# Expert 0's second product computed directly with 512-column products, the other experts' by seven block products

## The chip, the cores and the metric

The kernel runs on one NeuronCore of a Trainium2 chip. Its engines are TensorE (PE, matrix products), VectorE (DVE), ScalarE (ACT), GpSimd (POOL) and SyncE (SP, which here only issues transfers). Each runs its own instructions in the order in which the program wrote them; between engines, semaphores make one wait for another. The metric is the device time of one execution in microseconds (us), lower is better; the time of a version is the median of its runs.

## What is computed

The reference is a chunked attention followed by a mixture of eight experts whose weights come from a Sinkhorn routing:

```python
for c in range(nc):                      # attention: 4 batches, 8 heads, 768 rows, chunks of 32
    scores = scale * q_c @ k_full.T      # k_full: 8 memory rows and a window of 56
    out[c] = softmax(scores) @ v_full
x = out as [3072, 512]                   # all heads side by side
P = exp(x @ w_gate - max)                # then 8 rounds of row and column scaling
for e in range(8):
    h = np.maximum(x @ w1[e], 0.0)       # [3072, 1024]
    ye = h @ w2[e]                       # [3072, 512]
    out += P[:, e:e + 1] * ye
```

All data are float32. The kernel splits every operand of the expert products into a high and a low float16 part and multiplies three of the four pairs (`PASSES`), so one float32 product costs three float16 products.

## The kernel before

**Units.** The 3072 rows are cut into `NU` = 6 units of 512 rows (`TU` = 4 row tiles of 128). The work on the experts is a sequence of 48 units: expert 0 on units 0 to 5, expert 1 on units 5 to 0, and so on (L312). The hidden layer of a unit is computed in `FP` = 4 parts (`hidden`, L1275), the second product in two pairs of row tiles (`output`, L1473).

**Seven block products.** Both products are done as a 2 x 2 block product with seven multiplications in place of eight (`P1` to `P7`, L1244), which needs sums of blocks of both operands. For weights `cut` (L539) makes the sums on POOL (`ws`) and splits the plain blocks and the sums into high and low parts (`split`, L457: the high part on ACT, the low part on DVE). For the attention's result x the function `build` (L970) does the same, with its sums in `xt`, partly on DVE, partly on POOL. For the hidden layer the sums are made from the relu of the four blocks: `rr` and its negative on ACT (L1350, L1360), three steps on DVE (L1372), the high parts on ACT (L1383, L1408), the low parts on DVE (L1416) and, for the first `ASIDE` = 8 units, the low parts of the sums on POOL (L1432). Within a product, blocks gather in PSUM banks (px, py, pz and yx, yy, yz); ACT reads some of them into `q` or `y` (L1304, L1508), and DVE adds these to others (L1314, L1528).

**One stage with two kinds of work.** While expert 0 is computed, the attention still runs: 24 blocks of 128 rows, four to a unit. Each takes loads of q, k and v, transposes, scores (sp, L865), a softmax on DVE, ACT and POOL (the last step is L915), a transpose (ta) and the product with v (xp, L948). After every fourth block `build` makes the next unit's x and `logits` its router scores. After the last one comes the routing (L1135 to L1222), a chain between DVE and PE, and with it the first weights of expert 1.

**Who decides the order.** The kernel doesn't write its instructions in program order. Every step is a task of a `Plan` (L86) with an engine, an estimated cost and a due time (`prio`); `Plan.run` plays the tasks through with these estimates, on each engine takes the earliest due of those ready, and writes the instructions in the order that results. Where this leaves a hole on PE while the attention runs, `pad` (L119) fills it with products on a constant (`warm`, L376) that nobody reads. Due times follow from `begin(n)` (L314): START + TURN for each of the first five units, then UNIT for each, and `outputs_at(n)` (L319), half a TURN after a unit's begin for units 0 to 3. The attention's due times (`needed`, L625) follow START and AHEAD alone. `hidden` and `output` write their products through `product` (L1250), which makes each wait for the one before it through `last_pe`. For units 0 to 3 a unit's outputs come behind its hidden layer; from unit 5 on, the outputs of unit n - 1 come between the first and the second half of the hidden layer of unit n (L1682).

**Buffers.** A `Ring` (L53) hands out a few buffers in turn, in the order of the program's text; whoever takes one waits for all users of the tile that lay in it before. Of `ss` there are two, for the sums of h and for the attention's `xt`; of `c` there are two, for the three blocks of h before their split. x has two, h and the cut weights four each (more after the attention). PSUM gives `main` four banks.

**Results.** An expert adds its part to `acc`, which lies in DRAM between experts (`akeep`). Expert 0 stores its part unscaled, and expert 1 scales it when it fetches it (L1459).

Of the kernel before, what the change touches and what calls it, by code (L numbers as in the profile page):

```python
# [12 lines left out]
F32 = mybir.dt.float32  # L13
I32 = mybir.dt.int32
AF = mybir.ActivationFunctionType
ALU = mybir.AluOpType
# [69 lines left out]
class Plan:  # L86
# [13 lines left out]
    def add(self, eng, cost, fn, deps=(), prio=0.0, bufs=(), takes=None, frees=None, dma=0.0):  # L100
        t = Task()
        t.eng, t.cost, t.fn, t.prio, t.takes, t.frees = eng, cost, fn, prio, takes, frees
        t.ready, t.end, t.then, t.n, t.dma = 0.0, None, [], len(self.tasks), dma
        if dma:
            t.cost = cost * ISSUE
        before = {id(d): d for d in deps if d is not None}
        for b in bufs:
            assert not b.closed
            before.update({id(d): d for d in b.before})
            b.users.append(t)  # L110
        t.left = len(before)
        for d in before.values():
            d.then.append(t)
        if frees is not None:
            frees.left += 1
        self.tasks.append(t)
        return t
# [86 lines left out]
def tile_chunked_attn_sinkhorn_moe(  # L204
# [27 lines left out]
    nc = tc.nc  # L232
    P = 128
    B, H, S, D = q.shape
    NM = mem_k.shape[2]
    N, DM = out.shape
    E, _, F = w1.shape
# [11 lines left out]
    FP = F // P // 2  # L249
    GT = 256  # L250
# [3 lines left out]
    TU = UT // P  # L254
    TH = GT // P
    DH = DM // 2
    NBLK = B * NB
    SCALE = 1.0 / float(D) ** 0.5
    DOWN = 2.0**-HSHIFT
# [6 lines left out]
    hl = ctx.enter_context(tc.tile_pool(name="hl", bufs=1))  # L266
    stage = ctx.enter_context(tc.tile_pool(name="stage", bufs=1))
    apool = ctx.enter_context(tc.tile_pool(name="apool", bufs=1))
    comb = ctx.enter_context(tc.tile_pool(name="comb", bufs=1))
# [30 lines left out]
    akeep = [dram.tile([P, DM], F32, name=f"akeep_{T}") for T in range(NT)]  # L300

    plan = Plan()
    add = plan.add
# [2 lines left out]
    plan.free["two"] = [(0.0, 6)]  # L306


    START, TURN, UNIT, AHEAD = 50.0, 74.0, 36.7, 62.0
    ASIDE = NU + 2  # L310
    STEP = UNIT / 56
    units = [(e, u if e % 2 == 0 else NU - 1 - u) for e in range(E) for u in range(NU)]  # L312
# [39 lines left out]
    def buf(kind, pool, shape, dtype, name, slot=None):  # L352

        return rings[kind].take(
            lambda k: pool.tile(shape, dtype, tag=f"{kind}_{k}", name=name), slot
        )

    def operands(kind, shape, name):

        near = {"w1": wl1, "w2": wl2, "h": hl}[kind]  # L360
        return rings[kind].take(
            lambda k: (near if k < 4 else late[kind]).tile(
                shape, F16, tag=f"{kind}_{k}", name=name
            )
        )

    def bank(group, shape, name):
        return Bank(group, lambda b: ps.tile(shape, F32, tag=f"b{b}", name=name))

    FIRM = 200.0  # L370
# [86 lines left out]
    def split(dst, src, s, deps, prio, costs, bufs=()):  # L457

        a = add(
            "ACT",  # L460
            costs[0],
            lambda: nc.scalar.activation(dst(0), src(), AF.Copy, scale=s),  # L462
            deps,
            prio - 1.0,
            bufs,
        )
        b = add(
            "DVE",
            costs[1],
            lambda: nc.vector.scalar_tensor_tensor(  # L470
                dst(1), src(), s, dst(0), op0=ALU.mult, op1=ALU.subtract
            ),
            [a],
            prio,
            bufs,
        )
        return b
# [4 lines left out]
    wo = {}  # L482
    known = {}
# [54 lines left out]

    def cut(e, fp, which, st, ld, prio):  # L539
        s = sw[:, e, which - 1 : which]  # L540
        ws = buf(
            "ws", comb, [P, 4, 2, P] if which == 1 else [P, 4, DH], F32, f"ws{which}_{e}_{fp}"
        )
        eng = nc.gpsimd

        def tt(i, a, b, op):
            return lambda: eng.tensor_tensor(ws.t[:, i], a(), b(), op=op)  # L547

        def part(i):
            return lambda: ws.t[:, i]  # L550

        if which == 1:
            a11, a12 = lambda: st.t[:, 0, 0:2], lambda: st.t[:, 0, 2:4]
            a21, a22 = lambda: st.t[:, 1, 0:2], lambda: st.t[:, 1, 2:4]
            ops = [
                (0, a21, a22, ALU.add),
                (1, part(0), a11, ALU.subtract),
                (2, a11, a21, ALU.subtract),
                (3, a12, part(1), ALU.subtract),
            ]  # L560
            shape = [P, 2, 7, 2, P]
        else:
            b11, b12 = lambda: st.t[:, 1, 0:DH], lambda: st.t[:, 1, DH:DM]
            b21, b22 = lambda: st.t[:, 0, 0:DH], lambda: st.t[:, 0, DH:DM]
            ops = [
                (0, b12, b11, ALU.subtract),
                (1, part(0), b22, ALU.subtract),
                (2, b22, b12, ALU.subtract),
                (3, b21, part(1), ALU.add),
            ]  # L570
            shape = [P, 2, 7, DH]
        o = operands("w1" if which == 1 else "w2", shape, f"w{which}_{e}_{fp}")
        sums = []
        for op in ops:
            sums.append(add("POOL", 0.95, tt(*op), [ld] + sums[-1:], prio - 5, [st, ws]))
        deps = [known[e, which], ld]
        if which == 1:
            parts = [
                (
                    lambda j: o.t[:, j, 0:2].rearrange("p o k f -> p (o k) f"),  # L580
                    lambda: st.t[:, 0],
                    (0.72, 0.85),
                ),
                (lambda j: o.t[:, j, 2], a22, (0.5, 0.65)),
            ]
            flat = "p o k f -> p (o k f)"
        else:
            parts = [
                (
                    lambda j: o.t[:, j, 1:3].rearrange("p o d -> p (o d)"),  # L590
                    lambda: st.t[:, 0],
                    (0.72, 0.85),
                ),
                (lambda j: o.t[:, j, 0], b11, (0.5, 0.65)),
            ]
            flat = "p o d -> p (o d)"
        done = [split(d, src, s, deps, prio - 2, costs, [st, o]) for d, src, costs in parts]
        done.append(
            split(
                lambda j: o.t[:, j, 3:7].rearrange(flat),  # L600
                lambda: ws.t.rearrange(flat),
                s,
                deps + sums,
                prio,
                (1.15, 1.28),
                [ws, o],
            )
        )
        wo[e, fp, which] = (o, done)
# [636 lines left out]
    PASSES = ((0, 0), (0, 1), (1, 0))  # L1246
    now = [0.0, 1.0]
# [27 lines left out]
    def hidden(e, u, fp, hs, use_at, aside):  # L1275

        nm = f"{e}_{u}_{fp}"
# [3 lines left out]
        def run(dst, op, more, deps, takes=None):  # L1281
            a, b = op
            return product(
                dst,
                lambda: [
                    (w.t[:, wl, a, kt], x.t[:, xl, b, kt]) for kt in range(2) for wl, xl in PASSES
                ],
                more,
                deps,
                [w, x],  # L1290
                takes,
            )

        def psum(name):
            b = bank("main", [P, GT], f"{name}_{nm}")
            b.kind = "h"
            return b
# [12 lines left out]
        def plus(o, src, q, deps, last=True):  # L1310
# [10 lines left out]
            )  # L1321

        h = operands("h", [P, 2, 7, GT], f"h_{nm}")
        c = buf("c", comb, [P, 3, GT], F32, f"c_{nm}")
        px, py, pz = psum("px"), psum("py"), psum("pz")
        t1 = run(px, P1, False, made, px)
        q1, r1 = read(px, "q1", t1)
# [2 lines left out]
        c11 = plus(2, py, q1, [t2, r1])  # L1330
# [8 lines left out]
        c22 = plus(0, px, q5, [t7, r5], last=False)  # L1339
        yield  # L1340
        t3 = run(pz, P3, True, [r5])
        c12 = plus(1, pz, q6, [t3, r6])
        yield
        t4 = run(px, P4, True, [c22])

        rr = lambda i: h.t[:, 1, 3 + 2 * i : 5 + 2 * i].rearrange("p a n -> p (a n)").bitcast(F32)
        r = add(
# [5 lines left out]
            [h],  # L1353
            frees=px,
        )
        at = min(use_at, now[0] + 12.0)
        rn = add(
            "ACT",
            0.4,
# [6 lines left out]
        ss = buf("ss", comb, [P, 4, GT], F32, f"ss_{nm}")  # L1366

        def rsum(cost, dst, src, other, op, deps, extra=()):
# [11 lines left out]
        hi = add(  # L1380
            "ACT",
            0.85,
            lambda: nc.scalar.activation(h.t[:, 0, 0:3], c.t, AF.Relu),  # L1383
            [c11, c22, c12],
            at - 6.0,
            [h, c],
        )
# [33 lines left out]
                op0=ALU.max,  # L1421
                op1=ALU.subtract,
# [17 lines left out]
    akept = {}  # L1440
# [32 lines left out]
    def output(n, t, hs):  # L1473
# [135 lines left out]
            )  # L1609
        yield  # L1610


    def run(*gens):

        gens = list(gens)
        while gens:
            for g in list(gens):
                if next(g, StopIteration) is StopIteration:
                    gens.remove(g)

    def outputs(n, hs):
        run(*[output(n, t, hs) for t in range(TU // 2)])

    def first_weights():
# [19 lines left out]
        dma=0.3,  # L1644
# [3 lines left out]
    for n, (e, u) in enumerate(units):  # L1648
# [29 lines left out]
        hs = hidden_of[n] = []  # L1678
# [21 lines left out]
        if n >= NU and n % NU < NU - 2:  # L1700
# [16 lines left out]
                        dma=7.0,  # L1717
# [36 lines left out]
```

## Time and profile before

| | us |
|---|---|
| time, median of 3 runs | 2022.2 (2020.78 to 2023.33) |
| time of the profiled execution | 2018.44 |
| its span | 2016.6 |
| PE busy | 1956.9 |
| DVE busy | 1541.5 |
| ACT busy | 1065.8 |
| POOL busy | 625.0 |

The profile is of one execution. Its page has the busy time of each engine, the span in 40 slices of about 50 us with the busy share of each engine in tenths, the chain of work that ended last, and groups of instructions with a line of the kernel, an engine, what is written from what, a count, the busy time and the mean. A busy PE isn't a PE at its peak: products overlap, and a product's own length contains its passage through the array. A timeline lists instructions of one engine in order; its columns are start, length, engine, line, operation, tiles and count, and in brackets the idle time ahead of the first with what ended it. A table of windows gives the busy time of each engine in stretches of the span; restricted to a line or a tile, it gives those instructions alone.

### The profile page before, as it was taken

What the parts mean: (1) busy time and instruction counts of PE and PEld (TensorE: products, weight loads), DVE (VectorE), ACT (ScalarE), POOL (GpSimd) and SP (SyncE); (2) the same over time, 40 slices, a digit from 0 to 9 for tenths busy, and PEclk for the clock granted to TensorE, in tenths of its full rate; (3) what the DMA queues carried; (4) which work ended last, traced back from release to release, by engine and by line L of the source; (5) the groups of instructions that cost most, each with busy time, mean ns of one, the idle gap of its engine ahead of it and who ended that gap; (6) DMA issues with size and microseconds to landing.
All of it is one profiled execution on the core that took longest, in us unless ns stands there. A gap on an engine that the chain in (4) does not pass through costs nothing.

```text
span 2016.6 us, 48811 instructions
## 1 busy us (share of the span) xinstructions
PE 1956.9 (97%) x20193; PEld 1735.6 (86%) x20193; DVE 1541.5 (76%) x2522; ACT 1065.8 (53%) x2094; POOL 625.0 (31%) x608
## 2 busy tenths in 40 slices
PE   8889999989999999999999999999999999999999
PEld 7777878768888888888888888888888888888887
DVE  5997766798777886688867986788858977777564
ACT  4645655545555654554645555545536455465353
POOL 2543313246312422143223421242313521242112
PEclk9989999989999999999999999999999999999999
DMA  7664543025422544226423444146332453232321
GB/s 166 176 180 119 130 130 98 38 69 185 161 111 71 177 142 139 82 94 208 144 85 111 152 142 152 48 126 220 100 121 85 152 176 113 65 119 80 120 80 64
DMA packets 242191, 248.56 MB, mean 123 GB/s; under 512 B 114736, under 2 KB 176176, under 8 KB 237616
## 3 DMA queue, kind: packets, MB, share of 16 engines
q1 hardware_dynamic: 241328, 245.31, 38.2%
q8 instruction: 158, 2.59, 0.5%
q14 instruction: 65, 0.53, 0.1%
q10 hardware_dynamic: 640, 0.13, 0.0%
HBM read 184.04 MB, written 61.34 MB: 122 GB/s over the span
## 4 chain that ended last, share of the span: by engine, by line
PE 85%; DVE 10%; issue 2%; DMA 1%; POOL 1%; ACT 1%; SPq 0%; ACTq 0%; DVEq 0%; POOLq 0%
PE yx L1257 24%; PE px L1257 22%; PE yz L1257 12%; PE pz L1257 11%; PE yy L1257 6%; PE py L1257 6%; DVE ss L1372 3%; PE xp L948 2%; DVE c L1314 1%; DVE h L1416 1%; DVE w L470 1%; PE sp L865 1%; DVE x L470 1%; PE ta L938 1%; POOL h L1432 0%
## 5 line engine op out<-in xcount | busy, mean ns | idle before, releaser
L1257 PEld LDWEIGHTS <-w 128*128 128x128 f16 x8064 | 790.3, 98 | 120.0 <-issue 25.9
L1257 PEld LDWEIGHTS <-h 128*128 128x128 f16 x8064 | 789.8, 98 | 95.7 <-ACT h L1383 1.0
L1257 PE MATMUL px<-x,w 128*128 128x256 f16 x4608 | 566.7, 274 | 19.3 <-DVE c L1314 19.0
L1537 POOL TENSOR_TENSOR acc<-acc,y 128x256 f32<-128x256 f32 x252 | 274.6, 1095 | 891.5 <-ACT y L1512 888.4
L1257 PE MATMUL yx<-w,h 128*128 128x256 f16 x4608 | 538.4, 273 | 1.4 <-ACT h L1383 0.7
L1304 ACT ACTIVATE q<-px 128x256 f32<-128x256 f32 x384 | 146.3, 382 | 317.8 <-PE px L1257 311.4
L1257 PE MATMUL pz<-x,w 128*128 128x256 f16 x2304 | 284.8, 273 | 3.2 <-DVE c L1314 2.8
L1257 PE MATMUL yz<-w,h 128*128 128x256 f16 x2304 | 268.9, 273 | 0.0
L1383 ACT ACTIVATE h<-c 128x768 f16<-128x768 f32 x192 | 160.9, 838 | 126.0 <-DVE c L1314 125.8
L1408 ACT CAST h<-ss 128x1024 f16<-128x1024 f32 x192 | 199.1, 1040 | 39.6 <-DVE ss L1372 39.6
L1432 DVE TENSOR_TENSOR h<-ss,h 128x1024 f16<-128x1024 f32 x160 | 205.7, 1297 | 3.8 <-ACT h L1408 3.8
L1372 DVE SCALAR_TENSOR_TENSOR ss<-c,ss 128x256 f32<-128x256 f32 x384 | 199.9, 521 | 9.4
L1416 DVE SCALAR_TENSOR_TENSOR h<-c,h 128x768 f16<-128x768 f32 x192 | 196.0, 1024 | 12.8 <-ACT h L1383 12.7
L1314 DVE SCALAR_TENSOR_TENSOR c<-px,q 128x256 f32<-128x256 f32 x192 | 78.4, 422 | 111.7 <-PE px L1257 111.0
L1372 DVE SCALAR_TENSOR_TENSOR ss<-c,h 128x512 f32<-128x512 f32 x192 | 147.9, 770 | 7.5 <-ACT h L1360 7.3
L1257 PE MATMUL py<-x,w 128*128 128x256 f16 x1152 | 142.6, 274 | 0.0
L1512 ACT ACTIVATE y<-yx,pscale 128x256 f32<-128x256 f32 x168 | 79.6, 474 | 113.5 <-PE yx L1257 109.9
L1257 PE MATMUL yy<-w,h 128*128 128x256 f16 x1152 | 133.9, 273 | 0.0
L1314 DVE SCALAR_TENSOR_TENSOR c<-py,q 128x256 f32<-128x256 f32 x192 | 80.9, 424 | 63.8 <-PE py L1257 48.4
L1432 POOL TENSOR_TENSOR h<-ss,h 128x1024 f16<-128x1024 f32 x32 | 73.0, 2286 | 118.2 <-ACT h L1408 94.4
L462 ACT ACTIVATE w<-ws,sw 128x1024 f16<-128x1024 f32 x64 | 73.1, 1142 | 68.2 <-POOL ws L547 68.2
L470 DVE SCALAR_TENSOR_TENSOR w<-ws,sw,w 128x1024 f16<-128x1024 f32 x64 | 88.7, 1386 | 20.0 <-ACT w L462 20.0
(129 smaller groups left out, 1772.5 us busy)
## 6 DMA issues: line engine op xcount, KB each, us to landing
x<-xkeep SPq DMA_DIRECT2D x28, 1792.0 KB
akeep<-acc SPq DMA_DIRECT2D x168, 256.0 KB
acc<-akeep SPq DMA_DIRECT2D x168, 256.0 KB
w1f<-in_moe_w_dram SPq DMA_DIRECT2D x64, 256.0 KB
w2f<-in_moe_w_dram SPq DMA_DIRECT2D x32, 512.0 KB
w1fm<-in_moe_w_dram SPq DMA_DIRECT2D x56, 256.0 KB
w2fm<-in_moe_w_dram SPq DMA_DIRECT2D x28, 512.0 KB
xkeep<-x SPq DMA_DIRECT2D x6, 1792.0 KB
```

The source lines that it names most:

```text
L462: lambda: nc.scalar.activation(dst(0), src(), AF.Copy, scale=s),
L470: lambda: nc.vector.scalar_tensor_tensor(dst(1), src(), s, dst(0), op0=ALU.mult, op1=ALU.subtract),
L1257: nc.tensor.matmul(dst.t, a, b, start=(not more and n == 0), stop=(n == end), skip_group_check=more,)
L1304: lambda: nc.scalar.activation(t.t, src.t, AF.Copy, scale=DOWN),
L1314: lambda: nc.vector.scalar_tensor_tensor(c.t[:, o], src.t, DOWN, q.t, op0=ALU.mult, op1=ALU.add),
L1372: lambda: nc.vector.scalar_tensor_tensor(dst(), src(), 0.0, other(), op0=ALU.max, op1=op),
L1383: lambda: nc.scalar.activation(h.t[:, 0, 0:3], c.t, AF.Relu),
L1408: lambda: nc.scalar.copy(h.t[:, 0, 3:7], ss.t),
L1416: lambda: nc.vector.scalar_tensor_tensor(h.t[:, 1, 0:3].rearrange("p a n -> p (a n)"), c.t.rearrange("p a n -> p (a n)"), 0.0, h.t[:, 0, 0 ...
L1432: lambda: spare.tensor_tensor(h.t[:, 1, 3:7], ss.t, h.t[:, 0, 3:7], op=ALU.subtract),
L1512: (lambda: nc.scalar.activation(t.t, src.t, AF.Copy, scale=f))
L1537: lambda: nc.gpsimd.tensor_tensor(acc.t[:, cols], acc.t[:, cols], q.t, op=ALU.add),
```

## The change

For expert 0 alone the second product is done directly. `cut` then makes no sums of w2's blocks and splits the loaded tile as it is, 1024 columns at once. `hidden` keeps its seven products, but puts all four blocks of h in one tile `c` (from the ring `ss`) and splits their relu at once; sums, negative and POOL's step go. A new `plain_output` replaces `output`: for each row tile 24 products of 512 columns (four parts, two halves, three passes) gather in one PSUM bank, ACT copies it, and it is stored. These products don't go through `product`, so they aren't chained to `last_pe`; each part of six waits for its own h and w2. The other experts stay as they are. `TURN` goes from 74 to 68.

```diff
-    START, TURN, UNIT, AHEAD = 50.0, 74.0, 36.7, 62.0
+    START, TURN, UNIT, AHEAD = 50.0, 68.0, 36.7, 62.0
...
     def cut(e, fp, which, st, ld, prio):
         s = sw[:, e, which - 1 : which]
+        if e == 0 and which == 2:
+
+            o = operands("w2", [P, 2, 7, DH], f"w2_{e}_{fp}")
+            wide = "p a d -> p (a d)"
+            done = split(
+                lambda j: o.t[:, j, 0:4].rearrange(wide),
+                lambda: st.t.rearrange(wide),
+                s,
+                [known[e, 2], ld],
+                prio,
+                (1.15, 1.28),
+                [st, o],
+            )
+            wo[e, fp, 2] = (o, [done])
+            return
...
-        c = buf("c", comb, [P, 3, GT], F32, f"c_{nm}")
+
+        if e == 0:
+            c = buf("ss", comb, [P, 4, GT], F32, f"c_{nm}")
+        else:
+            c = buf("c", comb, [P, 3, GT], F32, f"c_{nm}")
...
         t4 = run(px, P4, True, [c22])
+        at = min(use_at, now[0] + 12.0)
+        if e == 0:
+            c21 = add(
+                "ACT",
+                0.4,
+                lambda: nc.scalar.activation(c.t[:, 3], px.t, AF.Copy, scale=DOWN),
+                [t4],
+                now[0] - FIRM,
+                [c],
+                frees=px,
+            )
+            hi = add(
+                "ACT",
+                1.07,
+                lambda: nc.scalar.activation(h.t[:, 0, 0:4], c.t, AF.Relu),
+                [c11, c22, c12, c21],
+                at - 6.0,
+                [h, c],
+            )
+            wide = "p a n -> p (a n)"
+            lo = add(
+                "DVE",
+                1.28,
+                lambda: nc.vector.scalar_tensor_tensor(
+                    h.t[:, 1, 0:4].rearrange(wide),
+                    c.t.rearrange(wide),
+                    0.0,
+                    h.t[:, 0, 0:4].rearrange(wide),
+                    op0=ALU.max,
+                    op1=ALU.subtract,
+                ),
+                [hi],
+                at - 5.0,
+                [h, c],
+            )
+            hs.append((h, [hi, lo], []))
+            yield
+            return
...
+    def plain_output(n, t, hs):
+
+        e, u = units[n]
+        T = u * TU + t
+        half, o = divmod(t * P, GT)
+
+        where = ((2, 3), (1, 0))[half]
+        a = buf("acc", apool, [P, DM], F32, f"acc_{e}_{T}")
+        py = bank("main", [P, DM], f"yp_{e}_{T}")
+
+        def part(fp):
+            def go():
+                hf, wf = hs[fp][0], wo[e, fp, 2][0]
+                for i, (fh, (hl, wl)) in enumerate(
+                    (fh, p) for fh in range(2) for p in PASSES
+                ):
+                    nc.tensor.matmul(
+                        py.t,
+                        hf.t[:, hl, where[fh], o : o + P],
+                        wf.t[:, wl, 2 * fh : 2 * fh + 2].rearrange("p a d -> p (a d)"),
+                        start=(fp == 0 and i == 0),
+                        stop=(fp == FP - 1 and i == 5),
+                    )
+
+            return go
+
+        t = None
+        for fp in range(FP):
+            t = add(
+                "PE",
+                1.3,
+                part(fp),
+                [t, *hs[fp][1], *wo[e, fp, 2][1]],
+                now[0],
+                [hs[fp][0], wo[e, fp, 2][0]],
+                takes=py if fp == 0 else None,
+            )
+            now[0] += 1.3 * now[1]
+        t = add("ACT", 0.6, lambda: nc.scalar.copy(a.t, py.t), [t], now[0] - FIRM, [a], frees=py)
+        akept[T] = add(
+            "SP", 1, lambda: nc.sync.dma_start(akeep[T], a.t), [t], now[0], [a], dma=1.3
+        )
...
     def outputs(n, hs):
+        if units[n][0] == 0:
+            for t in range(TU):
+                plain_output(n, t, hs)
+            return
         run(*[output(n, t, hs) for t in range(TU // 2)])
```

More of the change, by code (lines that the diff above doesn't have):

```diff
@@ L1355, in hidden @@
         )
-        at = min(use_at, now[0] + 12.0)
         rn = add(
```

## The prediction, made before the changed kernel had run

> **What bounds the kernel now.** I read the page first, its slices and its chain, then a table of windows over the stage that the change touches, and last the timeline where PE (TensorE) does no wanted work.
>
> ```profile
> span 2016.6 us, 48811 instructions
> PE   8889999989999999999999999999999999999999
> DVE  5997766798777886688867986788858977777564
> PE 85%; DVE 10%; issue 2%; DMA 1%; POOL 1%; ACT 1%; SPq 0%; ACTq 0%; DVEq 0%; POOLq 0%
> ...
> 1000.00:1200.00 200.00, 198.34 (x1816) 177.47 (x1815) 156.27 (x250) 103.86 (x202) 59.49 (x59) 1.00 0.36 123
> ```
>
> From the tenth slice on PE is full, and in 1000 to 1200 us it starts 1816 products in 200 us. Those later experts are not touched, so time can come only from the first quarter, where expert 0 runs beside the attention. I cut that stretch where PE passes from one unit's expert-0 work to the next; the columns are length, then PE, PE loads, DVE (VectorE), ACT (ScalarE) and POOL (GpSimd) busy, PE's clock, DMA.
>
> ```profile
> 62.50:144.80 82.30, 74.06 (x1036) 63.92 (x1033) 79.39 (x118) 46.87 (x90) 40.59 (x37) 0.92 0.66 179
> 144.80:208.30 63.50, 59.20 (x957) 51.26 (x956) 49.08 (x87) 35.15 (x76) 19.24 (x15) 0.97 0.57 146
> 208.30:278.00 69.70, 65.34 (x1150) 57.42 (x1148) 47.58 (x81) 38.48 (x82) 18.07 (x14) 0.98 0.44 115
> 278.00:342.70 64.70, 63.18 (x1051) 55.60 (x1040) 45.88 (x89) 37.49 (x79) 19.11 (x14) 1.00 0.46 122
> 342.70:385.60 42.90, 38.79 (x448) 32.69 (x446) 33.27 (x64) 21.84 (x43) 13.89 (x10) 0.92 0.02 8
> 385.60:444.70 59.10, 50.66 (x435) 43.43 (x434) 51.80 (x114) 31.94 (x62) 17.65 (x16) 0.91 0.26 86
> 444.70:488.10 43.40, 38.81 (x337) 33.56 (x336) 39.36 (x49) 22.84 (x45) 27.86 (x25) 0.96 0.54 177
> ```
>
> The first window (unit 0) is DVE's: 79.4 of 82.3 us. In the others nobody is full, so waits set the time. PE's busy figure counts filler products and overlapping tails, so I measure wanted work by starts:
>
> ```profile
> 209.10 2.06 PE L948 MATMUL xp<-at,v 64*64 64x32 f32 x64
> 211.09 0.66 PE L938 MATMUL ta<-ident,s 128*128 128x128 f32 x4
> 211.58 0.82 PE L1257 MATMUL px<-x,w 128*128 128x256 f16 x6
> ...
> 215.25 1.47 PE L1257 MATMUL py<-x,w 128*128 128x256 f16 x12
> 216.56 0.82 PE L1257 MATMUL px<-x,w 128*128 128x256 f16 x6
> 217.30 0.86 PE L865 MATMUL sp<-kC,qT 64*32 64x64 f32 x64
> 218.09 0.83 PE L1257 MATMUL px<-x,w 128*128 128x256 f16 x6
> ```
>
> Twelve 256-column products take 1.31 us from start to start, 0.1092 us each. An attention block takes 1.99 (xp) + 0.79 (sp) + three groups of transposes like ta's 0.49 = 4.25 us. By the code a unit has 168 + 168 products; the seven windows hold 2268 (expert 0's six units, and one and a half hidden phases of expert 1), 247.7 us, and 20 blocks, 85 us. Of 425.6 us that leaves **92.9 us** in which PE does nothing wanted, but for a few small products. By window, with 5, 14 and 1 blocks: unit 0 82.3 - 36.7 - 21.3 = 24.3; units 1 to 3 197.9 - 110.1 - 59.5 = 28.3, or 9.4 each; the next 42.9 - 18.3 - 4.3 = 20.3; the last two 102.5 - 82.6 = 19.9. Two holes stand out:
>
> ```profile
> 93.80 6.28 PE L376 MATMUL warm<-ident 128*128 128x256 bf16 x56
> 119.18 1.99 PE L1257 MATMUL yx<-w,h 128*128 128x256 f16 x12
> 366.54 4.09 PE L376 MATMUL warm<-ident 128*128 128x256 bf16 x36
> 385.65 1.47 PE L1257 MATMUL px<-x,w 128*128 128x256 f16 x12
> 114.19 4.21 POOL L1432 TENSOR_TENSOR h<-ss,h 128x1024 f16<-128x1024 f32 x2
> 118.58 1.23 DVE L470 SCALAR_TENSOR_TENSOR w<-ws,sw,w 128x1024 f16<-128x1024 f32 x1
> 369.68 2.29 POOL L1432 TENSOR_TENSOR h<-ss,h 128x1024 f16<-128x1024 f32 x1 [4.19 <-ACT h L1408]
> 372.05 0.79 POOL L1012 TENSOR_TENSOR xt<-xg 128x256 f32<-128x256 f32 x1
> 384.39 1.28 DVE L470 SCALAR_TENSOR_TENSOR x<-xt,sx,x 128x1024 f16<-128x1024 f32 x1
> ```
>
> In the first hole expert 0's first output waits for POOL's last low halves of h (to 118.4) and the last cut of w2 on DVE (to 119.8). In the second hidden(5) waits for x_5: its sums (xt) start only when POOL's low halves of unit 4 have freed the ring "ss" (the first xt starts 0.08 us behind an L1432), and its last split ends at 385.7.
>
> **The change part by part.** The profiled execution took 2018.4 us against a median of 2022.2, so I work out a difference on the former and add it to the latter.
>
> *More products.* A unit's output has 4 x 24 products of 512 columns for 168 of 256. At the row's 0.1092 per 256 columns that is 96 x 2 x 0.1092 = 20.97 for 18.35: 2.62 us a unit, **+15.7 us** on PE over six. Below, a 512-column product could cost less than two of 256 by whatever is fixed in each; above, nothing speaks for more, as a longer product hides its weight load better. I take 15.7. The Trainium skill ("TensorE: Matmul & The Clock Gate", section "Wait — 56ns, not 53.3ns?") gives a warm product as its columns at 2.4 GHz plus about 2.5 ns, 215.7 ns at 512. By it a unit would cost 20.7 us and the term +14.2 instead of +15.7; the 256-column row agrees with the rule (109.2 ns), no row here has 512.
>
> *Unit 0, DVE.* What goes, or shrinks, in that window:
>
> ```profile
> 62.50:144.80 82.30, 9.16 (x12) 0.92 0.66 179
> 62.50:144.80 82.30, 12.87 (x12) 4.35 (x8) 13.06 (x16) 0.92 0.66 179
> 62.50:144.80 82.30, 2.49 (x6) 0.92 0.66 179
> L1432 POOL TENSOR_TENSOR h<-ss,h 128x1024 f16<-128x1024 f32 x24 | 54.6, 2281 | 99.1 <-ACT h L1408 88.5 <-PE pz L1257 10.6
> 161.38 2.14 POOL L1432 TENSOR_TENSOR h<-ss,h 128x1024 f16<-128x1024 f32 x1 [0.57 <-ACT h L1408]
> 161.41 2.14 DVE L894 TENSOR_SCALAR sm<-sm 128x8 f32<-128x8 f32 x1
> L503 DVE TENSOR_REDUCE mxs<-w2f 128x1 f32<-128x1024 f32 x4 | 4.8, 1208 | 0.0
> L1416 DVE SCALAR_TENSOR_TENSOR h<-c,h 128x768 f16<-128x768 f32 x26 | 29.0, 1123 | 1.5 <-ACT h L1383 1.5
> ```
>
> The sums of h (L1372) were 9.2 us; of the 12.9 us on w2f the four maxima (4.8) stay and 8.1 us of cuts go, while the four 1024-wide cuts of ws become four of w2f itself; L1528's six adds were 2.5 us and become copies on ACT. The low halves (L1416) grow from 768 to 1024 columns, a third of 1.1 us, four times: +1.5. And an instruction of eight elements took 2.14 us because POOL's subtraction ran beside it; 24 of those, 54.6 us of POOL, go for expert 0. Without counting that, DVE needs 79.4 - 18.3 = 61 us; PE needs 36.7 + 2.6 + 21.3 = 60.6. The idle time lies between 24.3 (no gain) and nothing. I take what the next three windows show without DVE full, 9.4: **-14.9 us**.
>
> *Units 1 to 3.* The same sums and subtractions go (twelve of L1372 and four of L1432 a unit), and PE stood behind them only in part of 28.3 us; blocks waiting for loads or ACT stay. Between 0 and -28; I take a third, **-9.5**.
>
> *Unit 4's hole.* The output's products hung on one another through `last_pe`, behind hidden(5). The new ones wait for one h and one w2 each, and no hidden product waits for them: PE can do out(4)'s 20.97 us while x_5 is built. x_5 itself comes earlier, as its ring is freed by `lo` on DVE and not by POOL. Between 0 (the written order leaves out(4) behind hidden(5)) and -20.3; I leave 4 us for the first `lo`: **-16.3**.
>
> *The last two windows* hold routing and expert 1's first cuts on DVE, busy 51.8 of 59.1:
>
> ```profile
> 438.99 1.44 PE L1257 MATMUL px<-x,w 128*128 128x256 f16 x6 [3.43 <-DVE c L1314]
> ```
>
> PE waits there for DVE, which has eight h's less of sums and twelve adds less to do. Between 0 and -20; I take 40%, **-8.0**.
>
> *What costs nothing or moves.* On ACT an h loses two steps and an output six reads and copies a pair for four wider copies; both stand in the shade of PE: ACT is busy 35 of 63.5 us. `c` now lies in the ring that the attention's xt use; xt waits for `lo` where it waited for POOL, and behind it on POOL stands the attention's normalise. Loads and stores are as many as before: four stores of 256 KB a unit on SP, in another order. TURN moves due times by 6 us a unit: products step ahead of attention where both are ready, later experts move as a whole. I price it at nothing and give it 5 us either way, a row like 4.25 (one block too late).
>
> **Sum**: 15.7 - 14.9 - 9.5 - 16.3 - 8.0 = **-33.0 us**, 1985.4 for an execution like the profiled one, 1989 for the median. About 44 of the 92.9 us stay idle.
>
> **Rivals.** *PE closes up* (0.20). If POOL's subtractions were what slowed everything, idle falls to some 16 us: 15.7 - 77 = -61, 1961. For it: the 2.14 us pair above. By the Trainium skill ("SBUF — State Buffer", section "Who interferes with whom") the port pair of the two is an exclusive lock that one holds for a whole instruction, so up to all of POOL's removed time would be DVE's; the trace agrees at that pair. Against: half of the idle time in units 1 to 3 is not DVE's.
>
> *Gains fall short* (0.15). Out(4) stays behind hidden(5), since the plan thought x_5 ready, and DVE's relief only reaches unit 0: 15.7 - 14.9 - 5 = -4, 2018.
>
> *PE pays and the attention sets the pace* (0.10), slower. If units 0 to 3 wait for the attention's loads (DMA is busy 0.66 in unit 0, the most of all windows), DVE's freed time turns into waiting there. Only a part of unit 4's hole comes back, 8 us: 15.7 - 8 = +8, 2030. It decides from the point where less than 15.7 of the 92.9 us come back. Against: DVE, not PE or a queue, was full in that window.
>
> **How the numbers follow.** My forecast has 0.55, with 1974 to 2004 as its own range. The range is 1958 to 2014: it takes in the first rival and the better part of the second. A measurement of this kernel tells 0.2%, 4 us, from no change. Faster: 0.55 + 0.20 + 0.09 of the second = 0.84; same: 0.06 + 0.02 = 0.08; slower: 0.08.
>
> **What would show it.** Right: outputs of expert 0 at about 0.218 us a product; the first starts near 100 us; DVE in unit 0's window well under its length; out(4) before hidden(5) and few filler products there; expert 1 in full flow near 455 us instead of 488; the same 1816 products in 200 us afterwards. Wrong: PE idle before expert 0's outputs with a wait for v's loads or for xt; more than 70 us of idle left; a later stretch that lengthens because of another order.

## The result, and the profile after

The changed kernel takes **1967.5 us** (median of 4 runs, 1966.9 to 1968.3) against 2021.5 for the kernel before, measured beside it (2019.7 to 2023.3): a ratio of 0.9733, 95% interval 0.9716 to 0.9750, or 54.0 us less. Its profiled execution took 1967.2 us, with a span of 1965.5.

The stretch that the prediction cut into windows, in the profile of the changed kernel, cut at the same passages from one unit to the next. Columns as before: length, then PE, PE loads, DVE, ACT and POOL busy with instruction counts, PE's clock, DMA share, GB/s.

```profile
63.30:122.20 58.90, 58.11 (x737) 42.00 (x735) 52.10 (x81) 33.18 (x62) 13.34 (x13) 0.97 0.78 208
122.20:184.70 62.50, 62.09 (x1018) 46.54 (x1016) 42.24 (x77) 34.18 (x72) 12.35 (x15) 1.00 0.67 188
184.70:250.30 65.60, 65.45 (x1014) 48.65 (x1011) 35.48 (x64) 33.62 (x69) 10.78 (x11) 1.00 0.53 128
250.30:307.80 57.50, 56.17 (x849) 41.19 (x848) 33.91 (x60) 29.67 (x60) 9.31 (x9) 1.00 0.48 123
307.80:346.90 39.10, 39.10 (x533) 29.83 (x531) 25.65 (x48) 21.94 (x44) 6.77 (x7) 1.00 0.09 26
346.90:410.10 63.20, 62.73 (x428) 41.73 (x428) 54.98 (x122) 34.84 (x63) 20.41 (x22) 1.00 0.29 100
410.10:435.40 25.30, 19.15 (x170) 16.43 (x169) 24.22 (x33) 16.05 (x32) 12.26 (x11) 1.00 0.76 240
```

What took 425.6 us takes 372.1, and PE is now the busiest engine in six of seven windows (before: in four). Its clock is 0.97 in unit 0 and 1.00 after that, where it was between 0.91 and 1.00. DVE fell from 79.4 to 52.1 us in unit 0. Filler products (L376) fall from 33.4 to 2.8 us of PE over the seven windows. The timeline of PE shows the two old holes filled:

```profile
92.53 5.34 PE L1684 MATMUL yp<-w,h 128*128 128x512 f16 x24
...
336.57 1.47 PE L1684 MATMUL yp<-w,h 128*128 128x512 f16 x6
347.09 0.82 PE L1272 MATMUL px<-x,w 128*128 128x256 f16 x6
```

The first output starts at 92.5 us, not 119.2. Out(4) starts at 336.6, and 42 of its 96 products run before hidden(5) starts at 347.1. One long group of new products gives their price, from its start to that of the next:

```profile
399.76 10.52 PE L1684 MATMUL yp<-w,h 128*128 128x512 f16 x48
410.12 1.47 PE L1272 MATMUL px<-x,w 128*128 128x256 f16 x12
```

10.36 us for 48 is 0.2158 us each. With that, 0.1092 for a product of 256 columns and 4.25 for an attention block, wanted work by window is: unit 0 (4 blocks) 18.3 + 20.7 + 17.0 = 56.1 of 58.9; units 1 to 3 (14 blocks, 504 small and 283 large products) 175.6 of 185.6; the rest (2 blocks, 588 and 197) 115.2 of 127.6. **Idle time falls from 92.9 to 25.2 us.** In this count a product at a lower clock is idle time too. In the kernel before, one group of 24 took 4.20 us from start to start at a granted clock of 0.62, and a like one, two groups on, 2.62 at 1.00:

```profile
444.67 4.36 PE L1257 MATMUL yx<-w,h 128*128 128x256 f16 x24
448.87 2.78 PE L1257 MATMUL yy<-w,h 128*128 128x256 f16 x24
451.49 2.78 PE L1257 MATMUL yx<-w,h 128*128 128x256 f16 x24
454.11 2.78 PE L1257 MATMUL yz<-w,h 128*128 128x256 f16 x24
```

By the clocks of the windows this is at most about 20 us before (each window's length times what its clock lacks of 1.00) and 1.8 after. Behind the stretch hardly anything moved:

```profile
1000.00:1200.00 200.00, 198.33 (x1816) 177.47 (x1815) 154.63 (x247) 102.93 (x202) 64.05 (x66) 1.00 0.40 132
```

1816 products start in 200 us, as before. So the sum is 576 x (0.2158 - 0.1911) = +14.2 for the products (0.1911 is 168 x 0.1092 over 96) and -67.7 for idle time, -53.5 together. This is bookkeeping, since idle time is whatever the windows have left over: it says where the time went and not why. The spans of the two profiled executions differ by 51.1, as 0.8 us are lost ahead of the stretch and 1.6 behind it; the medians differ by 54.0.

### The profile page after: what moved, and what is told of

Its sections match the earlier page's. It is cut to its first block, busy times and chain, and to the rows that moved or that the text cites. A ratio compares the mean times of both kernels' runs of the same rounds, so it can differ in the third digit from the quotient of the medians.

```text
span 1965.5 us, 47252 instructions
## 1 busy us (share of the span) xinstructions
PE 1931.7 (98%) x19536; PEld 1665.8 (85%) x19536; DVE 1465.9 (75%) x2406; ACT 1031.5 (52%) x2014; POOL 557.3 (28%) x568
## 4 chain that ended last, share of the span: by engine, by line
PE 92%; DVE 6%; DMA 1%; issue 0%; SPq 0%; ACT 0%; POOL 0%; ACTq 0%; DVEq 0%; POOLq 0%
PE px L1272 24%; PE yx L1272 22%; PE pz L1272 12%; PE yz L1272 11%; PE py L1272 6%; PE yy L1272 6%; PE yp L1684 6%; PE xp L963 2%; DVE ss L1428 1%; DVE c L1329 1%; DVE w L470 1%; PE sp L880 1%; DVE x L470 1%; PE ta L953 1%; DVE h L1472 1%; PE warm L376 1%
## 5 line engine op out<-in xcount | busy, mean ns | idle before, releaser
L1272 PEld LDWEIGHTS <-h 128*128 128x128 f16 x7056 | 691.1, 98 | 82.7 <-ACT h L1439 1.0
L1272 PE MATMUL yx<-w,h 128*128 128x256 f16 x4032 | 469.6, 273 | 1.4 <-ACT h L1439 0.7
L1272 PE MATMUL yz<-w,h 128*128 128x256 f16 x2016 | 233.8, 273 | 0.0
L1439 ACT ACTIVATE h<-c 128x768 f16<-128x768 f32 x168 | 140.8, 838 | 113.2 <-DVE c L1329 113.2
L1464 ACT CAST h<-ss 128x1024 f16<-128x1024 f32 x168 | 174.1, 1039 | 15.7 <-DVE ss L1428 15.7
L1472 DVE SCALAR_TENSOR_TENSOR h<-c,h 128x768 f16<-128x768 f32 x168 | 168.3, 1005 | 11.7 <-ACT h L1439 11.6
L1428 DVE SCALAR_TENSOR_TENSOR ss<-c,ss 128x256 f32<-128x256 f32 x336 | 166.8, 496 | 8.0
L1428 DVE SCALAR_TENSOR_TENSOR ss<-c,h 128x512 f32<-128x512 f32 x168 | 129.7, 772 | 7.5 <-ACT h L1416 6.3
L1684 PE MATMUL yp<-w,h 128*128 128x512 f16 x576 | 132.0, 379 | 0.0
L1272 PE MATMUL yy<-w,h 128*128 128x256 f16 x1008 | 116.9, 273 | 0.0
L1684 PEld LDWEIGHTS <-h 128*128 128x128 f16 x576 | 55.2, 98 | 58.8 <-issue 0.8
```

What stands on the lines that cost most here:

```text
L1272: nc.tensor.matmul(dst.t, a, b, start=(not more and n == 0), stop=(n == end), skip_group_check=more,)
L1428: lambda: nc.vector.scalar_tensor_tensor(dst(), src(), 0.0, other(), op0=ALU.max, op1=op),
L1464: lambda: nc.scalar.copy(h.t[:, 0, 3:7], ss.t),
L1472: lambda: nc.vector.scalar_tensor_tensor(h.t[:, 1, 0:3].rearrange("p a n -> p (a n)"), c.t.rearrange("p a n -> p (a n)"), 0.0, h.t[:, 0, 0 ...
L1684: nc.tensor.matmul(py.t, hf.t[:, hl, where[fh], o : o + P], wf.t[:, wl, 2 * fh : 2 * fh + 2].rearrange("p a d -> p (a d)"), start=(fp == 0 ...
```

## The experiments

All times are medians, and differences are taken against the changed kernel's 1967.5 unless the kernel before is named. The question was whether the 67.7 us of idle time went because **DVE and POOL** do less (theory 1), because **outputs no longer hang in the chain** of hidden products (theory 2), or because of **TURN**. One limit holds for all: `Plan.run` writes another order for every version, and e1 and f4, which only move TURN between 74 and 68, moved by 5 us, so differences of that size are not put down to a cause. f2 and g1 do have the same order: apart from the added step itself, their traces show the same instructions one after the other on PE, DVE, ACT and POOL.

### TURN back at 74 (e1_turn74)

```diff
-    START, TURN, UNIT, AHEAD = 50.0, 68.0, 36.7, 62.0
+    START, TURN, UNIT, AHEAD = 50.0, 74.0, 36.7, 62.0
```

> The changed kernel with TURN back at 74. If the due times make the order that fills PE, some 15 to 30 us of the gain of 54 us go (1983 to 1998). If the gain comes from the work taken off DVE and POOL, or from outputs that no longer hang in one chain, TURN alone is worth less than 5 us either way (1963 to 1972).

Measured 1972.0, ratio to before 0.9755 (0.9740 to 0.9769): 4.6 us slower, at the edge of what was expected of a due time that does little.

### Outputs chained again (e2_chained)

```diff
-                [t, *hs[fp][1], *wo[e, fp, 2][1]],
+                [last_pe[0], *hs[fp][1], *wo[e, fp, 2][1]],
...
+            last_pe[0] = t
```

> The changed kernel, but the outputs of expert 0 are chained to the hidden products again, as they were before; the lighter DVE and POOL work stays. Theory 1 (relief of DVE and POOL carries the gain): only unit 4's hole comes back, 10 to 20 us slower than the changed kernel (1978 to 1988). Theory 2 (PE gains because outputs can go into any hole): 30 to 50 us slower (1998 to 2018).

Measured 1974.6, 0.9766 (0.9750 to 0.9782): only 7.1 us slower, less than either theory said and not far above the 5 us of a mere reordering. PE's timeline of this run at the old second hole, and the last split of x_5:

```profile
336.50 1.47 PE L1272 MATMUL px<-x,w 128*128 128x256 f16 x12
...
343.43 3.77 PE L376 MATMUL warm<-ident 128*128 128x256 bf16 x33
347.04 0.82 PE L1272 MATMUL px<-x,w 128*128 128x256 f16 x6
350.39 0.27 PE L443 MATMUL row_lg<-ident,most_of 128*1 128x128 f32 x1 [2.54 <-DVE most_of L1159]
348.09 1.27 DVE L470 SCALAR_TENSOR_TENSOR x<-xt,sx,x 128x1024 f16<-128x1024 f32 x1
```

The hole is there again, but it is half as long: hidden(4)'s last product starts at 336.5 and ends it near 338, and hidden(5) starts at 347.0, some 9 us later, where before it came 19 us later (366.5 to 385.7). With less on DVE and POOL, x_5 is ready at 349.4 us and not at 385.7, so that even a chained output leaves little open.

### POOL's subtraction back, and which part of it costs (e3_pool_back, f2_pool_free, g1_pool_memset)

e3 adds, for each of expert 0's 24 parts of h, a subtraction like the old one; nobody reads it. In f2 it reads h in place of c. In g1 two fills take its place.

```diff
+            add(
+                "POOL",
+                2.3,
+                lambda: nc.gpsimd.tensor_tensor(
+                    h.t[:, :, 4:6],
+                    c.t.rearrange("p (a b) n -> p a b n", a=2),
+                    h.t[:, 0, 0:4].rearrange("p (a b) n -> p a b n", a=2),
+                    op=ALU.subtract,
+                ),
+                [hi],
+                at - 1.0,
+                [h, c],
+            )
             hs.append((h, [hi, lo], []))
```

In f2 the second operand line is the third once more and the buffers are `[h]`. In g1 the step is this, with `[h]` too:

```diff
+                lambda: [nc.gpsimd.memset(h.t[:, :, 4:7], 0.0) for _ in range(2)],
```

> The changed kernel with a POOL subtraction of 1024 columns for each of expert 0's 24 parts of h added back; nobody reads its result, but the buffer c is held until it is done. 24 times 2.3 us on POOL. Theory 1: DVE and the attention's sums are held up again, 15 to 30 us slower (1983 to 1998). Theory 2: PE has other work in the meantime, less than 5 us.

> As e3_pool_back, but POOL's subtraction reads h alone, so that it holds no buffer that the attention's sums wait for; its result is unread. If e3's 23.6 us came from the two engines standing in each other's way, nearly all of it stays (1983 to 1992). If they came from the ring, whose buffers POOL then gave back late, less than 8 us stay (1967 to 1975).

> The changed kernel with two fills of 1536 half-precision columns on POOL for each of expert 0's parts of h in place of the subtraction of f2; they read no memory. If e3 and f2 lost 23.6 us because POOL is late for the attention's own steps, a like time on POOL costs as much here (1983 to 1992). If they lost them because DVE stands while POOL reads, nearly nothing is lost (1965 to 1973), and DVE's eight-element steps stay at 0.17 us.

e3 takes 1991.1 (0.9846, 0.9829 to 0.9863), 23.6 us more; f2 1991.9 (0.9856, 0.9833 to 0.9878), the same. So the ring isn't what makes the subtraction dear. g1 takes 1978.8 (0.9793, 0.9776 to 0.9809), 11.3 us more: between its two expectations. The groups of instructions in the first 450 us (line, engine, operation, shapes, count, busy us, mean ns) show what differs. The changed kernel:

```profile
L1387 DVE SCALAR_TENSOR_TENSOR h<-c,h 128x1024 f16<-128x1024 f32 x24 | 30.0, 1257 | 11.3 <-ACT h L1378 10.9
L909 DVE TENSOR_SCALAR sm<-sm 128x8 f32<-128x8 f32 x24 | 4.1, 172 | 0.8
```

f2, with the subtraction:

```profile
L1402 POOL TENSOR_TENSOR h<-h 128x1024 f16<-128x1024 f16 x24 | 61.3, 2567 | 61.5 <-ACT h L1378 59.3 <-PE tq L817 2.2
L1387 DVE SCALAR_TENSOR_TENSOR h<-c,h 128x1024 f16<-128x1024 f32 x24 | 42.7, 1789 | 6.1 <-ACT h L1378 6.0
L909 DVE TENSOR_SCALAR sm<-sm 128x8 f32<-128x8 f32 x24 | 9.9, 414 | 0.8
```

g1, with the fills:

```profile
L1402 POOL MEMSET h<- 128x1536 f16 x48 | 65.5, 1377 | 1.4
L1387 DVE SCALAR_TENSOR_TENSOR h<-c,h 128x1024 f16<-128x1024 f32 x24 | 30.7, 1289 | 6.1 <-ACT h L1378 6.0
L909 DVE TENSOR_SCALAR sm<-sm 128x8 f32<-128x8 f32 x24 | 4.9, 203 | 0.8
```

Both load POOL for over 60 us. While POOL subtracts, DVE's split of h takes 1.79 us on average in place of 1.26 and its step on eight elements a row (L909) 0.41 in place of 0.17; while POOL fills, they take 1.29 and 0.20. The Trainium skill ("SBUF — State Buffer", section "Who interferes with whom") says that a DVE instruction with two SBUF inputs contends with a GpSimd instruction that reads SBUF and not with one that only writes it. The split, which reads c and h, agrees with that. The eight-element step reads one tile, which that sentence doesn't cover, and it slows all the same.

Since f2 and g1 have one order and load POOL alike, the 13.1 us between them, over half of f2's loss, go with DVE being held up. The 11.3 us between g1 and the changed kernel are another matter: there the order differs too. PE's waits from 63 us on (what waits for what: us in total, times, longest), of the changed kernel first and then of g1:

```profile
PE px L1272 <- DVE w L470: 0.2, 1, 0.2
```

```profile
PE px L1272 <- DVE w L470: 6.7, 2, 3.6
PE ta L953 <- POOL s L930: 0.5, 2, 0.4
```

PE hardly waits for the attention's step on POOL (0.5 us), and g1's last attention block comes only 2.7 us later than the changed kernel's (337.2 for 334.6). Most of the loss lies behind it, where PE waits 6.7 us in all for splits of expert 1's weights. Whether POOL's time or the other order made these late was not tried.

### DVE's sums back, and all of it back (e4_sums_back, g2_pool_sums, f1_all_back)

```diff
+            for cost, dst, a, b in (
+                (0.72, lambda: h.t[:, 1, 4:6].rearrange(flat2), (0, 2), (2, 4)),
+                (0.47, lambda: h.t[:, 1, 6], (0, 1), (1, 2)),
+                (0.47, lambda: h.t[:, 0, 6], (2, 3), (3, 4)),
+            ):
+                add(
+                    "DVE",
+                    cost,
+                    lambda dst=dst, a=a, b=b: nc.vector.scalar_tensor_tensor(
+                        dst(),
+                        c.t[:, a[0] : a[1]].rearrange(flat2),
+                        0.0,
+                        c.t[:, b[0] : b[1]].rearrange(flat2),
+                        op0=ALU.max,
+                        op1=ALU.add,
+                    ),
+                    [c11, c22, c12, c21],
+                    at - 4.0,
+                    [h, c],
+                )
```

g2 has this and e3's edit, f1 these two and e2's chain.

> The changed kernel with three DVE sums for each of expert 0's 24 parts of h added back (512, 256 and 256 columns, some 1.6 us a part, 38 us in all); nobody reads them, but c is held until they are done. Theory 1: 10 to 25 us slower (1978 to 1993), most of it in unit 0, where DVE is busy 52 of 59 us. Theory 2: less than 5 us.

> The changed kernel with POOL's subtraction and DVE's sums both back, the outputs still free of the chain. If the two add up, 37 us slower than the changed kernel (2001 to 2008). If they feed one another, 42 to 53 us (2010 to 2020). Against f1 (2027.3) it shows what the chain costs where DVE and POOL are loaded: 7 us if the chain is worth the same everywhere.

> The changed kernel with all three put back: outputs chained, POOL's subtraction and DVE's three sums for each part of h (their results unread). If the three add up, 7.1 + 23.6 + 13.4 = 44 us slower than the changed kernel, 2012. If they hide one another, 23 to 35 us (1991 to 2003). If they feed one another, 50 to 65 us (2017 to 2033), which is the kernel before plus the dearer products.

e4 takes 1980.9 (0.9805, 0.9785 to 0.9825), 13.4 us more. The size is as expected, the place isn't: it was to be unit 0. Counted at the prices above, PE has done 340 us of wanted work at 406.3 us in e4 and at 404.5 in the changed kernel, but 360 us at 439.6 and 428.5; in between PE waits for splits of expert 1's weights, as in g1. g2 takes 2028.8 (1.0032, 1.0017 to 1.0047), **61.3 us more**, where 23.6 and 13.4 add up to 37: together they cost more than apart, beyond the 42 to 53 that were written for that case. f1 takes 2027.3 (1.0032, 1.0021 to 1.0043): once both are back, the chain makes no difference. The rows for DVE's 256-column sums and its split, of e4 and then of g2, and for g2 POOL's subtraction:

```profile
L1408 DVE SCALAR_TENSOR_TENSOR h<-c 128x256 f16<-128x256 f32 x48 | 21.4, 473 | 0.0
L1387 DVE SCALAR_TENSOR_TENSOR h<-c,h 128x1024 f16<-128x1024 f32 x24 | 29.5, 1234 | 1.0 <-ACT h L1378 0.8
```

```profile
L1408 DVE SCALAR_TENSOR_TENSOR h<-c 128x256 f16<-128x256 f32 x45 | 33.9, 779 | 0.0
L1387 DVE SCALAR_TENSOR_TENSOR h<-c,h 128x1024 f16<-128x1024 f32 x24 | 45.3, 1897 | 0.6
L1423 POOL TENSOR_TENSOR h<-c,h 128x1024 f16<-128x1024 f32 x24 | 61.7, 2586 | 79.0 <-ACT h L1378 79.0
```

The added sums (0.47 us alone) take 0.78 beside POOL, and the split 1.90 for 1.23: DVE gets more work, and POOL stretches the added work as well. POOL's subtraction itself is no longer than in e3 (2.59 us for 2.71). With 2028.8 the sums and the subtraction together are enough to eat the whole gain. Nobody reads their results, so what they bring back is the load on the two engines and not a wait for the sums. They are not the old kernel over again: the last attention block's product starts at 371.2 us in g2 and at 353.3 before, and the steps that ACT was spared were not put back by any run.

### Part of the change in the kernel before (f3_before_unchained, f4_before_turn68)

f3 gives `output` for expert 0 a chain of its own; f4 sets TURN to 68.

```diff
-    def product(dst, pairs, more, deps, bufs=(), takes=None):
+    own_pe = [None]
+
+    def product(dst, pairs, more, deps, bufs=(), takes=None, last_pe=last_pe):
...
                 [h[0] for h in hs] + [w[0] for w in ws],
                 takes,
+                own_pe if e == 0 else last_pe,
```

> The kernel before, with one edit: expert 0's outputs hang on one another alone and not on the hidden products. If the chain were what kept PE idle, 20 us or more faster than before (below 2001). If DVE and POOL hold the data up, what e2 showed or less: 0 to 10 us faster (2011 to 2021).

> The kernel before with TURN 68 alone. Due times alone free no engine: within 5 us of before (2016 to 2026). If they made the order that fills PE, 15 us or more faster (below 2006).

f3 takes 2017.0 beside 2020.8 for before (0.9976, 0.9964 to 0.9989), 3.8 us faster; f4 2015.9 (0.9977, 0.9967 to 0.9986), 4.9 faster. Neither the freed order nor the due times, each alone, fill PE while the old work stays on DVE and POOL.

### The cuts of w2 back (g3_cut_back)

The extra work of the old cuts is added for expert 0's w2: four POOL sums into `ws` and two more splits for each part, unread.

```diff
+            for i, a, b, op in (
+                (0, b12, b11, ALU.subtract),
+                (1, lambda: ws.t[:, 0], b22, ALU.subtract),
+                (2, b22, b12, ALU.subtract),
+                (3, b21, lambda: ws.t[:, 1], ALU.add),
+            ):
...
+            split(
+                lambda j: o.t[:, j, 4:6].rearrange(wide),
+                lambda: st.t[:, 0],
...
+            split(
+                lambda j: o.t[:, j, 6],
+                lambda: st.t[:, 1, 0:DH],
...
             wo[e, fp, 2] = (o, [done])
```

> The changed kernel with the extra work of w2's old cuts back for expert 0 (four times four POOL sums and two more splits on ACT and DVE), unread. It falls into unit 0's window alone: 5 to 10 us slower (1972 to 1978) if that window is DVE's, less than 3 us if PE sets it.

Measured 1974.1 (0.9771, 0.9756 to 0.9786): 6.7 us more for 16 POOL sums and eight more splits, the size that was expected of a window that is DVE's. The trace puts most of it elsewhere. Hidden(1), which starts at 122.2 us in the changed kernel, starts here at 124.5, and a longer wait follows in unit 1:

```profile
124.53 1.47 PE L1312 MATMUL px<-x,w 128*128 128x256 f16 x12
...
153.16 1.12 PE L993 MATMUL ta<-ident,s 128*128 128x128 f32 x4 [3.24 <-POOL s L970]
```

There the softmax's last step on POOL is late; why was not followed up, and 6.7 us are not far from what a mere reordering does. So this run doesn't show that unit 0 is still DVE's.

### TURN 62 (g4_turn62)

> The changed kernel with TURN 62. About 25 us of idle PE are left beside the attention and after it. If due times still cost something, 2 to 5 us faster than the changed kernel (1962 to 1966); if 68 suits, within 2 us or slower (1966 to 1975).

Measured 1989.7 (0.9845, 0.9830 to 0.9860): **22.2 us slower**, which neither side expected. The timeline has the last attention block's product with v, of the changed kernel and then of g4:

```profile
334.58 2.06 PE L963 MATMUL xp<-at,v 64*64 64x32 f32 x64
```

```profile
358.22 2.05 PE L963 MATMUL xp<-at,v 64*64 64x32 f32 x64
```

It comes 23.6 us later, and the whole time grows by 22.2. The attention's due times follow AHEAD, 62; with TURN at 62 the products fall due as fast as the attention does and go first, so that expert 0 is left waiting for an x that is late. The chain that ended last bears this out. In g4 it runs through x's splits on DVE at three unit changes and at the end; in the changed kernel, from 63 us on, only near 287 us. First g4, then the changed kernel:

```profile
120.11 4.59 DVE x L470 x6
246.81 4.12 DVE x L470 x6
310.83 4.13 DVE x L470 x6
363.97 5.32 DVE x L470 x7
```

```profile
287.32 5.32 DVE x L470 x7
```

That it is the distance between TURN and AHEAD was not tried, as AHEAD was not varied. None of the versions beats the changed kernel.

## Why the prediction was right, and where its sizes were off

The forecast was 1989 with a range of 1958 to 2014; measured were 1967.5. That is outside the forecast's own 1974 to 2004; the range holds it because it took in the first rival. Direction and place were right: expert 0's stage, idle PE time, nothing behind it. The size was too small by 21 us. Step by step:

- **More products**, +15.7 by the row of 256 columns: +14.2 by the measured 0.2158 us. The estimate from the Trainium skill's rule for a warm product ("TensorE: Matmul & The Clock Gate", section "Wait — 56ns, not 53.3ns?"), +14.2, was the right one of the two; the run agrees with it.
- **Unit 0**, -14.9: its idle time fell from 24.3 to 2.8, -21.5. This is a term that was mis-sized. It took the idle time of units 1 to 3 (9.4) as what would stay, but that fell too (to 10.0 for the three) once DVE and POOL had less to do, so it was no floor.
- **Units 1 to 3**, -9.5: idle time fell from 28.3 to 10.0, -18.3. This is the other mis-sized term. "PE stood behind them only in part" was the step that failed: DVE wasn't full there (46 to 49 us of 64 to 70), but POOL's subtractions stretched its steps. e3 and g2 show what that was worth over the whole stage: 23.6 us alone, 61.3 together with the sums. "Half of the idle time in units 1 to 3 is not DVE's" had no row behind it, and nearly two thirds of it went.
- **Unit 4's hole and the last two windows**, -16.3 and -8.0: idle time fell from 40.2 to 12.4, -27.8. Split at 346.9 us, these are -18.6 and -9.2, so both sizes are about right. The weight of the reasons for the first is not. The prediction closed the hole chiefly with outputs that leave the chain and named an earlier x_5 without a price. In e2 the chain is worth 7.1 us; half of the hole had gone with the outputs still chained, since x_5 was built sooner.
- **What costs nothing**: moving TURN by 6 us was given 5 us either way. Between 74 and 68 that holds (4.6 us, and 4.9 in f4). From 68 to 62 it doesn't.
- **A reading**: the cut of w2 that ends at 119.8 us can't have held the first output's first products, which start at 119.2. Nothing in the sum hangs on it.
- **The rivals.** "PE closes up", 1961 with a chance of 0.20, came within 7 us, but in part by luck. It put everything down to POOL's subtractions, and e3 gives 23.6 us for these alone; it took DVE's sums as well to bring back the whole. Its idle rest was set at 16 us, and 25 stayed. That gains would fall short is refuted by the time and by out(4), whose first 42 products run ahead of hidden(5); that the attention's loads would set the pace, by unit 0's window, which shrank with DMA at 0.78.

## What to carry to other kernels

Fewer multiplications are a gain only where the matrix engine is what runs out: here seven block products in place of eight saved 14 us of PE, and work like the sums that they need, put back on DVE and POOL, cost 61 us, in the one stage where these two had other work. Moving a step to an idle engine need not be free: POOL was never full here, and a subtraction on it that reads cost 13 us more than fills of about the same length, through DVE. So price such a step as time on both. And idle time in a window where no engine is full is no floor; look for steps there that take longer than their shortest case.

## What was not expected of the hardware

DVE's eight-element step took 0.17 us in the changed kernel, 0.20 on average with POOL filling and 0.41 to 0.46 with POOL subtracting (f2, e3). 61 us of subtractions cost 24 us of the kernel's time. 66 us of fills in the same order of instructions cost 11.
